# The chunk loop of a linear recurrence with two MLP stages: its steps in another order

## The chip, the cores and the metric

The kernel runs on one core of a Trainium2 chip. The metric is the device time of one execution in microseconds; the time before is the median of three runs.

## The reference

Two things follow each other. The first is a recurrence over 768 time steps, for 4 x 8 heads with a 40 x 40 state each:

```python
for t in range(S):
    y[:, :, t] = np.einsum('bhd,bhde->bhe', rt, state)
    Sa = np.einsum('bhde,bhe->bhd', state, at)
    state_decay = state * wt[:, :, None, :] - np.einsum('bhd,bhe->bhde', Sa, bt)
    state = state_decay + np.einsum('bhd,bhe->bhde', vt, kt)
```

Its output, 3072 tokens of 320 features, goes through two MLPs: `elu(x @ w_in) @ w_out` with 2048 hidden features, then `max(x @ w1, x @ w2, x @ w3) @ w_out` with 768 hidden features. All is in fp32 (the weights come as 64-bit numbers).

## The kernel before, in words

The recurrence is done in 24 chunks of 32 time steps. In a chunk, the 32 heads lie side by side in small blocks, and the steps inside the chunk are solved as a triangular system. The first MLP runs beside it: TensorE works on its 128 x 256 pieces between the small steps of the recurrence. The second MLP runs when the recurrence has ended.

Every engine takes its instructions in the order in which the program writes them (`tc.manual_schedule()`), so the order of calls in the chunk loop is the order of each engine's queue. A chunk `c` has eight segments `s0` to `s7`. In segment `n` these are written one behind another:

- the segment's own steps, `s()`;
- `KP[n]` steps of the generator `stK(c + 1)`, which turns the K and B data of the next chunk (tile KT) into YL: per half one 32 x 32-block transpose on VectorE (tile psK in PSUM), then four steps of two copies each on ScalarE; at `n == 5` what is left of it is flushed, and the next KT is loaded;
- what `CHAIN` says for the loads, stores and statistics of the triangular solve, which itself runs on GpSimd;
- where `n` is in `LT` (from chunk 4 on), one tick of `later`, the conversion of the second MLP's weights: four ticks a weight piece, each of one or two VectorE passes, some with a DMA, a sum of absolute values (Abs) on ScalarE, or both;
- two fills: one `fc1` (eight matmuls into `h`, then an exp on ScalarE and, for an older piece, a cast) and one `fc2` (six matmuls into `acc`, then two VectorE passes on an `e`, called elu here, and a subtraction on GpSimd).

The steps of the recurrence in chunk `c` are, with `d = c + 2`:

- `stU`, `stT1`, `stX`, `stT2`, `stS`: the chain of the state. psU is copied to Us by ScalarE, psV likewise to v; psX is added to Us by VectorE (L337); psT is copied to VSI by ScalarE (four copies); psS is multiplied into US by VectorE (four passes, L358).
- `stR(c, h)`: transposes one half of US through psR, in two tiles of eight, and ScalarE copies them (L371) into YL of the next chunk. psS of the next chunk reads them.
- `stN`: transposes VSI through psN; ScalarE copies it to VN. `stG` multiplies VN with Rbd, VectorE masks the result into GR. `stY` and `stY2` make the output of the chunk before (Yt on VectorE, then a split into two parts and DMAs to DRAM).
- `prep1a`, `prep1b`, `prep2`, `prep3`, `prep_stat`: scans (Q, Pt), the products Abd (one half for each of two values of `par`, L177) and KT (two halves, L185) on VectorE, and two passes with an accumulated sum over Q and Pt on ScalarE (L195).
- `stA(d, h)`: multiplies KT with Abd into psA; VectorE masks psA into AK (L201), then ScalarE copies parts to NB and Abd to AK.

All PSUM tiles of the recurrence (psU, psV, psX, psT, psA, psK, psS, psR, psN, psG, psY) share four buffers of the pool `ps`. The tiles h have two buffers, acc two.

Of the kernel before, what the change touches and what calls it, by code (L numbers as in the profile page):

```python
# [7 lines left out]
F32 = mybir.dt.float32  # L8
# [25 lines left out]
ST = ((3, 3, 2, 3, 3, 2, 3, 3), (2, 2, 3, 3, 3, 3, 4, 4))  # L34
NW = 8
NF = 8
LT = (1, 3, 4, 6, 7)
N3, N1 = 34, 22
NPC = N3 + N1
KD = 3  # L40
K0 = (0, 0, 2, 2, 2, 2, 2, 2)
KP = (0, 1, 1, 1, 2, 1, 2, 2)
FL = ((0, 0, 0, 0, 2, 2, 2, 2), (2, 2, 2, 2, 2, 2, 2, 2), (2, 2, 2, 2, 2, 2, 2, 2), (2, 2, 2, 2, 2, 2, 2, 2))


# [11 lines left out]
def _main(tc, io, out, bad):  # L57
# [4 lines left out]
    with ExitStack() as outer, tc.manual_schedule():  # L62
# [27 lines left out]
        r1 = rec.enter_context(tc.tile_pool(name="r1", bufs=1))  # L90
# [23 lines left out]
        def load_wa(c):  # L114
            if c < NCH:
                wa = r1.tile([104, 1056], F32, tag="wa", name="wa")
                sp.dma_start(wa[:], io["wa"][c])
                wt[c], at[c] = wa, wa[:, 544:]
# [10 lines left out]
        def load_vsi(c):  # L129
            if c < NCH:  # L130
                sp.dma_start(VSI[0:32].rearrange("p a b e -> p (a b e)"), io["vt"][c])
# [41 lines left out]
        def prep2(c, par):  # L173
            if c >= NCH:
                return
            sl = slice(64 * par, 64 * par + 40)
            nc.vector.tensor_tensor(  # L177
                out=Abd[sl, par], in0=at[c][sl, :].rearrange("p (a b) -> p a b", b=32),
                in1=Pt[c][sl, :, 0:32], op=mult,
            )  # L180
# [50 lines left out]
        def stK(c):  # L231
            if c >= NCH:
                return
            new_YL(c)
            for h in range(2):
                if c < KD:
                    q = [ps.tile([64, 8, 40], F32, tag="ps", name="psK") for _ in range(2)]
                    for p in range(8):
                        for par in range(2):
                            sl = slice(64 * par, 64 * par + 40)  # L240
                            nc.tensor.transpose(q[par][:, p], KB[c][sl, 8 * h + p].rearrange("r a b -> r (a b)"),
                                                ident[sl, sl])
                    yield
                    for par in range(2):
                        nc.scalar.copy(YL[c][0:64, 8 * h:8 * h + 8, par], q[par][:])
                        yield
                    continue
                q = ps.tile([128, 8, 2, 32], F32, tag="ps", name="psK")
                nc.vector.transpose(out=q[:].rearrange("r p k t -> r (p k t)"),  # L249
                                    in_=KT[c % 2][:, 8 * h:8 * h + 8].rearrange("r p k t -> r (p k t)"))  # L250
                yield
                for par in range(2):
                    for e0, n in ((0, 32), (32, 8)):
                        for k in range(2):
                            nc.scalar.copy(YL[c][32 * k:32 * k + 32, 8 * h:8 * h + 8, par, e0:e0 + n],  # L255
                                           q[64 * par + e0:64 * par + e0 + 32, :, k, 0:n])
                        yield
# [54 lines left out]
        def stU(c):  # L312
            q = ps.tile([128, 8, 40], F32, tag="ps", name="psU")
            for g in range(8):
                for k in range(4):
                    par, p = head(k, g)
                    nc.tensor.matmul(q[32 * k:32 * k + 32, g], AK[c][:, par, p], US[:, p, par],
                                     start=True, stop=True)
            QQ["us"] = us = r1.tile([128, 8, 40], F32, tag="Us", name="Us")
            nc.scalar.copy(us[:], q[:])  # L320
# [13 lines left out]
        def stX(c):  # L334
            q = ps.tile([128, 8, 40], F32, tag="ps", name="psX")
            blocks(q, NB[c % 3], QQ["v1"], 16)
            nc.vector.tensor_tensor(out=QQ["us"][:], in0=q[:], in1=QQ["us"][:], op=add)  # L337
            nc.scalar.activation(out=QQ["v1"][:, :, 0:32], in_=NB[c % 3][:], func=ACTF.Abs,
                                 accum_out=stat[:, c, 4:5])
# [8 lines left out]
        def stS(c, h):  # L348
            if c + 1 >= NCH:
                return  # L350
            q = ps.tile([104, 8, 40], F32, tag="ps", name="psS")
            for p in range(8):
                for par in range(2):
                    nc.tensor.matmul(q[64 * par:64 * par + 40, p], YL[c][:, 8 * h + p, par],
                                     VSI[:, 8 * h + p, par], start=True, stop=True)
            for par in range(2):
                sl = slice(64 * par, 64 * par + 40)
                nc.vector.tensor_tensor(  # L358
                    out=US[64:104, 8 * h:8 * h + 8, par], in0=q[sl],
                    in1=PC[c + 1][sl, 8 * h:8 * h + 8].to_broadcast([40, 8, 40]), op=mult,  # L360
                )
# [11 lines left out]
        def stN(c):  # L373
            q = ps.tile([80, 16, 32], F32, tag="ps", name="psN")
            for p in range(16):
                nc.tensor.transpose(q[:, p], VSI[32:64, p].rearrange("r a e -> r (a e)"), ident[32:64, 32:64])
            nc.scalar.copy(VN[:, :, 1], q[:])
# [364 lines left out]
        for c in range(NCH):  # L742
            d = c + 2 if c else NCH
            def s0():
                if c:
                    stU(c)
                    stY(c - 1)
                    load_gr(c)
                load_us(c + 1)
                prep1b(d)  # L750

            def s1():
                stT1(c)
                if c:
                    stY2(c - 1)
                prep2(d, 0)
                prep2(d, 1)

            def s2():
                stX(c)  # L760
                load_wa(d + 1)
                prep3(d, 0)
                prep3(d, 1)

            def s3():
                stT2(c)
                stA(d, 0)
                stA(d, 1)

            def s4():  # L770
                stS(c, 0)
                stS(c, 1)
                load_vsi(c + 1)

            def s5():
                stN(c)
                prep_stat(d)

            def s6():
                stR(c, 0)  # L780
                stG(c, 0)
                stG(c, 1)
                load_g(c + 1)

            def s7():
                stR(c, 1)
                prep1a(c + 3)

            segs = (s0, s1, s2, s3, s4, s5, s6, s7)
            if c == 3:  # L790
                qw[0] = sp
            sk = stK(c + 1)
            for n, s in enumerate(segs):
                if c == 2 and n == LX:
                    tick(99)
                    tick(1, second)
                if n == 2 and c >= 2 and c % 2 == 0:
                    state["x", c // 2 - 1] = load_x(c // 2 - 1)
                if n == (DN if c > 2 else D2) and c >= 2 and c % 2 == 0:
                    done[0] = c // 2  # L800
                if c > 1 and n == 3:
                    for _ in sv:
                        pass
                    solve_store(c + 1)
                s()
                for _ in range(KP[n] if c + 1 >= KD else K0[n]):
                    next(sk, None)
                if n == 5:
                    for _ in sk:
                        pass  # L810
                    load_kb(c + 3)
                for f, k in CHAIN[min(c, 2)].get(n, ()):
                    chain[f](c + k)
                if c < 2:
                    if ("load", 2) in CHAIN[c].get(n, ()):
                        for _ in solve(c + 2):
                            pass
                else:
                    if n == 7:
                        sv = solve(c + 2)  # L820
                if c < 2 or c == 2 and n < LX:
                    tick(FT[c][n])
                elif c < 4:
                    tick(ST[c - 2][n], second)
                if c == 3 and n == 7:
                    tick(1, later)
                if c > 3 and n in LT:
                    tick(1, later)
                for _ in range(FL[(c > 2) + (c > 3) + (c == NCH - 1)][n] if c > 1 else 0):
                    fill()  # L830
                    next(sv, None)
                    next(sv, None)
# [362 lines left out]
```

## Time and profile before

| | |
|---|---|
| median of three runs | 1109.33 us (1108.91 to 1109.74) |
| the profiled execution, its time | 1110.41 us |
| its span, first to last instruction | 1108.5 us |
| TensorE matmul busy | 968.2 us (87%) |
| VectorE busy | 702.3 us (63%) |
| ScalarE busy | 587.2 us (53%) |
| GpSimd busy | 443.0 us (40%) |
[...]

Busy shares are means over the whole span. The chunk loop is over at about 760 us, the rest of the first MLP at about 826 us, and behind that lies the second MLP. In the profile PE is the matmul engine, PEld its weight load, DVE is VectorE, ACT ScalarE, POOL GpSimd, SP the queue that issues most DMAs. Names such as L337 are lines of the kernel. A releaser, behind "<-", is the instruction whose end let the waiting one start.

### The profile page before, as it was taken

The page shows a single profiled execution, that of the slowest core. Times are in us where ns is not written, and L with a number is a line of the kernel's source. Part 1 is how long each engine was busy: PE and PEld are TensorE (multiplying, and loading weights), DVE is VectorE, ACT ScalarE, POOL GpSimd, SP SyncE. Part 2 cuts the span into 40 slices and gives each one's busy share as a digit, 9 for nine tenths or more (in the row PEclk, how much of TensorE's full clock was granted, in tenths as well). Part 3 has the DMA queues.
Part 4 walks back from the last instruction along what each step waited for, and adds up shares of the span by engine and source line. Part 5 has one row for each costly group of instructions (what it writes and reads, how often), then busy time and mean ns, then how long its engine had stood idle before and what let it go on. Part 6 is the DMA issues. An engine that isn't in the chain of part 4 may idle for free.

```text
span 1108.5 us, 38422 instructions
## 1 busy us (share of the span) xinstructions
PE 968.2 (87%) x15992; PEld 863.5 (78%) x15992; DVE 702.3 (63%) x1368; ACT 587.2 (53%) x1705; POOL 443.0 (40%) x952
## 2 busy tenths in 40 slices
PE   2255697998999988899999898999999999999996
PEld 2154587888888887788888887888998888888885
DVE  7979786777777877877677777775433333333321
ACT  3466655776776666667667666775332212122121
POOL 3542264665656666655556666653330000000000
PEclk9965578999998999999889999999999999999998
DMA  6854554664555556545545555542581001010000
GB/s 170 218 149 128 128 138 97 158 144 118 138 149 138 139 139 153 140 116 126 141 121 146 131 137 143 142 125 74 178 231 28 29 26 53 1 53 24 1 24 27
DMA packets 187430, 125.27 MB, mean 113 GB/s; under 512 B 125770, under 2 KB 167498, under 8 KB 187122
## 3 DMA queue, kind: packets, MB, share of 16 engines
q1 hardware_dynamic: 174123, 104.66, 37.8%
q10 hardware_dynamic: 13127, 18.09, 5.4%
q8 instruction: 128, 2.10, 0.8%
q14 instruction: 52, 0.43, 0.1%
HBM read 92.82 MB, written 29.88 MB: 111 GB/s over the span
## 4 chain that ended last, share of the span: by engine, by line
PE 45%; DVE 27%; DMA 8%; ACT 8%; issue 4%; POOL 4%; SPq 2%; ACTq 0%; POOLq 0%; DVEq 0%
PE psh L881 18%; PE h L566 7%; PE acc L600 6%; PE acc L903 5%; ACT YL L255 3%; PE psA L215 3%; DVE e L578 3%; DVE e L577 2%; DVE US L358 2%; DVE Abd L177 2%; DVE KT L185 2%; DVE Yt L398 2%; DVE Pt L166 2%; DVE psK L249 2%; DVE AK L201 2%
## 5 line engine op out<-in xcount | busy, mean ns | idle before, releaser
L566 PE MATMUL h<-x,W 128*128 128x256 f32 x1536 | 243.6, 303 | 12.4 <-DMA x<-dX 6.7
L587 POOL TENSOR_TENSOR g<-e,g 128x256 fp32r<-128x256 f32 x192 | 156.8, 817 | 237.1 <-DVE e L577 108.5
L566 PEld LDWEIGHTS h<-x,W 128*128 128x128 f32 x1536 | 204.9, 197 | 23.2 <-issue 8.3
L881 PE MATMUL psh<-xT,V 128*128 128x512 f32 x864 | 212.3, 397 | 0.8 <-ACT xT L872 0.7
L600 PE MATMUL acc<-W2h,g 128*128 128x320 f32 x768 | 204.4, 315 | 0.4 <-POOL g L587 0.4
L881 PEld LDWEIGHTS psh<-xT,V 128*128 128x128 f32 x864 | 159.4, 188 | 34.9 <-ACT xT L872 1.0
L284 POOL TENSOR_TENSOR tmp<-WT,X 128x15 f32<-128x15 f32 (+4 forms) x360 | 125.4, 348 | 97.9 <-ACT raw L443 25.9
L577 DVE TENSOR_SCALAR e<-e 128x256 f32<-128x256 f32 x192 | 69.5, 362 | 143.4 <-ACT e L570 143.3
L886 DVE TENSOR_TENSOR mx<-psh,mx 128x512 f32<-128x512 f32 x72 | 49.8, 692 | 159.2 <-PE psh L881 159.1
L600 PEld LDWEIGHTS acc<-W2h,g 128*128 128x128 f32 x768 | 140.8, 194 | 3.2 <-issue 2.0
L286 POOL TENSOR_TENSOR WT<-WT,tmp 128x15 f32<-128x15 f32 (+4 forms) x360 | 129.7, 360 | 28.2
L600 PE MATMUL acc<-W2l,g 128*128 128x320 f32 x384 | 121.0, 315 | 2.4 <-issue 2.4
L889 ACT CAST g<-mx 128x512 fp32r<-128x512 f32 x36 | 22.3, 620 | 173.1 <-DVE mx L886 173.1
L570 ACT ACTIVATE e<-h 128x256 f32<-128x256 f32 x192 | 73.5, 383 | 72.4 <-PE h L566 47.9
L255 ACT COPY YL<-psK 32x256 f32<-32x256 f32 (+1 forms) x336 | 95.2, 283 | 30.1 <-DVE psK L249 25.9
L578 DVE TENSOR_TENSOR e<-h,e 128x256 f32<-128x256 f32 x192 | 81.5, 425 | 6.6
L215 PE MATMUL psA<-Abd,KT 104*64 104x64 f32 x768 | 46.1, 278 | 39.8 <-DVE KT L185 37.3
L583 ACT CAST g<-e 128x256 fp32r<-128x256 f32 x192 | 76.3, 398 | 0.6 <-DVE e L578 0.3
L600 PEld LDWEIGHTS acc<-W2l,g 128*128 128x128 f32 x384 | 74.6, 194 | 0.0
L215 PEld LDWEIGHTS psA<-Abd,KT 104*64 104x64 f32 x768 | 39.6, 186 | 44.4 <-ACT W L468 21.6
L903 PE MATMUL acc<-O,g 128*128 128x320 f32 x432 | 69.2, 308 | 0.1
L903 PEld LDWEIGHTS acc<-O,g 128*128 128x128 f32 x432 | 66.2, 188 | 3.5 <-DVE g L890 0.4
(123 smaller groups left out, 1468.0 us busy)
## 6 DMA issues: line engine op xcount, KB each, us to landing
wa<-in_wa SPq DMA_DIRECT2D x24, 429.0 KB
KT<-in_kbT SPq DMA_DIRECT2D x23, 416.0 KB
rawv<-in_wv SPq DMA_DIRECT2D x18, 384.0 KB
X<-dN SPq DMA_DIRECT2D x96, 64.0 KB
x<-dX SPq DMA_DIRECT2D x24, 256.0 KB
V<-dV SPq DMA_DIRECT2D x6, 960.0 KB
raw<-in_w ACTq DMA_DIRECT2D x7, 768.0 KB
US<-in_vt SPq DMA_DIRECT2D x24, 160.0 KB
```

The lines of the kernel that those rows point to most:

```text
L215: nc.tensor.matmul(q[64 * u:64 * u + 64, p], KB[c][:, 8 * u + p].rearrange("r a b -> r (a b)"), Abd[:, :, 8 * u + p], start=True, stop=True)
L255: nc.scalar.copy(YL[c][32 * k:32 * k + 32, 8 * h:8 * h + 8, par, e0:e0 + n], q[64 * par + e0:64 * par + e0 + 32, :, k, 0:n])
L284: eng.tensor_tensor(out=tv, in0=Wt[:, 0:nu, s:s + 1].to_broadcast([128, nu, n]), in1=X[:, s:s + 1, s + 1:16].to_broadcast([128, nu, n]), o ...
L286: eng.tensor_tensor(out=Wt[:, 0:nu, s + 1:16], in0=Wt[:, 0:nu, s + 1:16], in1=tv, op=sub)
L566: nc.tensor.matmul(h, W1[:, wi, 128 * m:128 * m + 128], x[:, xi], start=(n == 0), stop=(n == 7))
L577: nc.vector.tensor_scalar(out=e[:], in0=e[:], scalar1=1.0, scalar2=-1.0, op0=ALU.min, op1=add)
L578: nc.vector.tensor_tensor(out=e[:], in0=h, in1=e[:], op=ALU.max)
L583: nc.scalar.copy(gt[i][:, 0], es[i][:])
L587: nc.gpsimd.tensor_tensor(out=gt[i][:, 1], in0=es.pop(i)[:], in1=gt[i][:, 0], op=sub)
L600: nc.tensor.matmul(acc[t][:], g[:, gi, ts], w[:, m], start=(m == 0 and n == 0), stop=(m == 15 and n == 2))
L881: nc.tensor.matmul(q[:], V[:, w, wi, ms], xT[:, hl, k], start=(n == 0), stop=(n == 7))
L903: nc.tensor.matmul(acc[t], g[:, gi, ts], O[:, wi, m], start=(m == 0 and n == 0), stop=(m == 5 and n == 2))
```

## The change

- The transposes of KT write to a tile `ks` in SBUF, with one buffer, in place of a PSUM buffer of `ps`.
- The second half of Abd (`prep2(d, 1)`) moves from segment 1 to segment 2, behind `stX`.
- `stN` moves from segment 5 to the end of segment 4, behind both halves of `stS`.
- The second half of `stR` moves from segment 7 to the start of the next chunk's segment 0.
- The steps of `stK` are spread otherwise: segment 3 has two and segment 4 one, and the flush goes from segment 5 to segment 7. The load of the next KT stays at segment 5.
- The ticks of the weight conversion stand in segments 2, 4, 5, 6, 7 in place of 1, 3, 4, 6, 7.

```diff
--- before.py
+++ after.py
@@ -34,12 +34,12 @@
 ST = ((3, 3, 2, 3, 3, 2, 3, 3), (2, 2, 3, 3, 3, 3, 4, 4))
 NW = 8
 NF = 8
-LT = (1, 3, 4, 6, 7)
+LT = (2,4,5,6,7)
 N3, N1 = 34, 22
 NPC = N3 + N1
 KD = 3
 K0 = (0, 0, 2, 2, 2, 2, 2, 2)
-KP = (0, 1, 1, 1, 2, 1, 2, 2)
+KP = (0, 1, 1, 2, 1, 1, 2, 2)
 FL = ((0, 0, 0, 0, 2, 2, 2, 2), (2, 2, 2, 2, 2, 2, 2, 2), (2, 2, 2, 2, 2, 2, 2, 2), (2, 2, 2, 2, 2, 2, 2, 2))
 
 
@@ -245,7 +245,7 @@
                         nc.scalar.copy(YL[c][0:64, 8 * h:8 * h + 8, par], q[par][:])
                         yield
                     continue
-                q = ps.tile([128, 8, 2, 32], F32, tag="ps", name="psK")
+                q = r1.tile([128, 8, 2, 32], F32, tag="ks", name="ks")
                 nc.vector.transpose(out=q[:].rearrange("r p k t -> r (p k t)"),
                                     in_=KT[c % 2][:, 8 * h:8 * h + 8].rearrange("r p k t -> r (p k t)"))
                 yield
@@ -743,6 +743,7 @@
             d = c + 2 if c else NCH
             def s0():
                 if c:
+                    stR(c - 1, 1)
                     stU(c)
                     stY(c - 1)
                     load_gr(c)
@@ -754,10 +755,10 @@
                 if c:
                     stY2(c - 1)
                 prep2(d, 0)
-                prep2(d, 1)
 
             def s2():
                 stX(c)
+                prep2(d, 1)
                 load_wa(d + 1)
                 prep3(d, 0)
                 prep3(d, 1)
@@ -770,10 +771,10 @@
             def s4():
                 stS(c, 0)
                 stS(c, 1)
+                stN(c)
                 load_vsi(c + 1)
 
             def s5():
-                stN(c)
                 prep_stat(d)
 
             def s6():
@@ -783,7 +784,6 @@
                 load_g(c + 1)
 
             def s7():
-                stR(c, 1)
                 prep1a(c + 3)
 
             segs = (s0, s1, s2, s3, s4, s5, s6, s7)
@@ -806,9 +806,10 @@
                 for _ in range(KP[n] if c + 1 >= KD else K0[n]):
                     next(sk, None)
                 if n == 5:
+                    load_kb(c + 3)
+                if n == 7:
                     for _ in sk:
                         pass
-                    load_kb(c + 3)
                 for f, k in CHAIN[min(c, 2)].get(n, ()):
                     chain[f](c + k)
                 if c < 2:
```

## Rows read from the trace of the kernel before

**Rows 1.** stretches: from:to, length, PE PEld DVE ACT POOL busy, clock, DMA, GB/s
```profile
184.60:733.10 548.50, 502.13 (x10950) 455.30 (x10948) 418.15 (x801) 376.39 (x1143) 330.44 (x706) 0.95 0.55 135
704.90:733.10 28.20, 26.24 (x592) 23.65 (x588) 21.73 (x46) 21.05 (x66) 17.80 (x42) 1.00 0.54 129
733.10:758.70 25.60, 25.20 (x580) 22.95 (x580) 18.73 (x39) 16.72 (x51) 15.08 (x37) 1.00 0.49 130
```

**Rows 2.** waits of TensorE, 200 to 780 us: total us, times, longest
```profile
PE psT L326 <- DVE Us L337: 21.1, 14, 2.8
PE psR L370 <- ACT YL L371: 8.5, 13, 0.7
PE psA L215 <- DVE KT L185: 5.3, 13, 0.7
```

**Rows 3.** waits of VectorE, 200 to 780 us
```profile
DVE e L577 <- ACT e L570: 114.6, 47, 3.6
DVE AK L201 <- PE psA L215: 17.1, 17, 1.4
```

**Rows 4.** timeline of VectorE, 591 to 615 us: start, us, what, idle before
```profile
599.06 0.29 DVE L577 TENSOR_SCALAR e<-e 128x256 f32<-128x256 f32 x1 [2.40 <-ACT e L570]
...
601.89 0.70 DVE L448 SCALAR_TENSOR_TENSOR cf<-rawv 128x384 fp32r<-128x384 f32 x1
...
603.18 0.72 DVE L249 STREAM_TRANSPOSE psK<-KT 128x512 f32<-128x512 f32 x1
606.72 0.29 DVE L577 TENSOR_SCALAR e<-e 128x256 f32<-128x256 f32 x1 [2.83 <-ACT e L570]
```

**Rows 5.** timeline of ScalarE, 591 to 615 us
```profile
598.20 0.42 ACT L255 COPY YL<-psK 32x64 f32<-32x64 f32 x2
598.64 0.38 ACT L570 ACTIVATE e<-h 128x256 f32<-128x256 f32 x1
...
599.49 1.18 ACT L255 COPY YL<-psK 32x256 f32<-32x256 f32 x4
...
601.26 0.59 ACT L377 COPY VN<-psN 80x512 f32<-80x512 f32 x1
601.74 0.65 ACT L195 ACTIVATE Q<-Q 104x528 f32<-104x528 f32 x1
...
603.92 2.35 ACT L255 COPY YL<-psK 32x256 f32<-32x256 f32 x8 [0.68 <-DVE psK L249]
```

**Rows 6.** chain that ended last, 520 to 650 us: start, us, what
```profile
593.20 1.16 PE psA L215 x30
...
619.26 1.62 DVE rawv L436
...
623.91 1.74 PE psA L215 x30
```

**Rows 7.** groups by line: busy us, mean ns, idle before
```profile
L185 DVE TENSOR_TENSOR KT<-KT,Q 104x512 f32<-104x512 f32 x48 | 40.5, 883 | 0.1
...
L177 DVE TENSOR_TENSOR Abd<-wa,Pt 40x512 f32<-40x512 f32 x48 | 35.8, 747 | 0.3
...
L225 ACT COPY AK<-Abd 40x512 f32<-40x512 f32 x48 | 29.6, 617 | 0.8
...
L377 ACT COPY VN<-psN 80x512 f32<-80x512 f32 x24 | 14.0, 582 | 4.3 <-PE psN L376 4.3
```

**Rows 8.** timeline of TensorE, 591 to 615 us
```profile
602.45 0.75 PE L370 MATMUL psR<-ident,US 40*40 40x40 f32 x16
```

**Rows 9.** timeline of TensorE, 556 to 572 us
```profile
561.31 0.79 PE L326 MATMUL psT<-Us,TB 32*32 32x40 f32 x64 [1.88 <-DVE Us L337]
...
563.04 1.97 PE L215 MATMUL psA<-Abd,KT 104*64 104x64 f32 x30 [0.68 <-DVE KT L185]
564.95 2.08 PE L566 MATMUL h<-x,W 128*128 128x256 f32 x8
...
570.34 1.22 PE L566 MATMUL h<-x,W 128*128 128x256 f32 x8
```

## The prediction

> **What bounds the kernel now.** I read the stretches first. The steady chunks c = 4 to 21 take 184.6 to 733.1 us [rows 1]: 548.5 / 18 = 30.47 us a chunk. After that TensorE is all but full (25.20 us busy of 25.60 in chunk 22 [rows 1]) and nothing there is touched, so a gain has to come out of those 18 chunks. The chunk from 704.9 ran wholly at the full clock and was 28.20 us long with 26.24 us of TensorE work [rows 1]; TensorE therefore could do a chunk in some 26.3 us, and about 4.2 us of each chunk are waits and half clock.
>
> The waits of TensorE tell where [rows 2], over 19 chunks: psT for Us (the psX add on VectorE) 21.1 us, psR for a copy of an older psR 8.5, psA for KT 5.3. It looks as if the late add were the fault. But why is VectorE late? Its own waits [rows 3] are 114.6 us, 6.0 a chunk, for the exp on ScalarE. The timeline of one chunk names two places [rows 4]: 2.40 us before the elu of segment 3 and 2.83 us before that of segment 5. ScalarE's timeline [rows 5] shows what it did meanwhile: before the first it runs the copies of AK and then two of YL, before the second the flush of eight YL copies, 2.35 us from 603.92, which stand in its queue ahead of segment 5's exp.
>
> So I read the chunk as a ring on VectorE and ScalarE. The chain of waits runs from psA at 593.20 to psA at 623.91 [rows 6], 30.71 us: psA, AK masks (VectorE), NB and AK copies, YL copies, exp (ScalarE), elu, US, convert tick, elu, psK transpose (VectorE), YL flush, exp (ScalarE), then without a break on VectorE elu, GR, tick, elu, Q, tick, elu, Yt, Pt, elu, Abd, psK, tick, elu, the add, KT, and psA again. What shortens this ring shortens the chunk; what only moves TensorE's wait within it does not.
>
> **The change part by part**, costed in this ring.
>
> *The add above Abd's second half.* The add now comes one Abd half (0.75 us [rows 7]) sooner, and the tick that stood ahead of it is gone from segment 1. psT starts earlier and its wait shrinks. But psA needs the second Abd half and both KT products (0.88 us each [rows 7]), and these now stand behind the add: VectorE runs the same instructions before psA as before. In the ring: 0. TensorE's wait goes from psT to psA.
>
> *The YL flush leaves segment 5.* The exp of segment 5 no longer stands behind eight copies. VectorE's 2.83 us go, if that exp is ready when VectorE gets there. In the row's chunk ScalarE now ends exp and cast of segment 3 at 599.49, where the next copies start, and would end them at 599.49 + 0.90 = 600.4 (the 0.90 is the next two items). Then come VN 0.59, a YL pair 0.42, exp and cast of segment 4 some 0.7, both statistics 603.92 - 0.68 - 601.74 = 1.50 and an exp 0.38 [rows 5]: ready at 604.0. VectorE would be there at 603.18 + 0.72 [rows 4] + 0.90 = 604.8 plus a tick. The margin is 0.8 us and the tick. Gain 2.83. The copies go to segments 6 and 7, where ScalarE loses no time of VectorE: the exps are wanted there after GR, Q and ticks.
>
> *One more YL step in segment 3.* KP[3] becomes 2, so one more pair, 1.18 - 0.42 = 0.76 us [rows 5], runs ahead of the exp for which VectorE already waits 2.40. Loss 0.76.
>
> *KT's transposes into SBUF.* ScalarE now reads its source from SBUF. The nearest pair of rows, both 512 elements, is 617 ns from SBUF against 582 from PSUM [rows 7]: 35 ns a copy, four in segment 3, loss 0.14; the other twelve lie in cover. [...] The transpose itself on VectorE, 0.72 us into PSUM [rows 4], has no row into SBUF. Bounds: 0.56 (an SBUF to SBUF pass over 256 elements takes 0.29 [rows 4], doubled) and 0.88 (KT, two SBUF inputs, 512 elements [rows 7]). It streams one input of the same 512 elements, so I take 0.72; two of them in the ring make the range +-0.32 a chunk.
>
> *The ticks.* Segments 1, 3, 4, 6, 7 become 2, 4, 5, 6, 7. The one in 1 moves to 5: both lie in the ring, 0. The one in 3 ran inside the 2.40 us wait, free; in 2 it stands between KT and the AK masks, where VectorE waits for psA 17.1 / 17 = 1.0 us [rows 3]. A tick takes 0.70 to 1.62 us and more [rows 4, 6], about 1.0 on average; where psA is quick it spills over. Loss 0 to 0.6, taken 0.3. The tick's weight load (SP) and stores (ScalarE's queue) move with it by one or two segments; a piece is loaded one piece, four ticks, ahead, so nobody waits.
>
> *psN beside psS; psR's second half in the next chunk.* psN's 16 transposes and the VN copy move up; 16 transposes of psR, 0.75 us [rows 8], and two copies move into the next chunk's start, ahead of psU. Neither issues a DMA, and GpSimd's and SP's queues keep their order. The next half of psR no longer waits for a PSUM buffer, nor does KT's transpose hold one: TensorE's 8.5 us [rows 2] go, but TensorE is not the ring, and the gain is 0. Behind the moved copies on ScalarE stand Us and the exp of segment 0; VectorE gets to that exp only after Yt and Pt. If that cover were gone they would cost two copies, some 0.8 us.
>
> Sum: 2.83 - 0.76 - 0.14 - 0.3 = 1.63 us a chunk; 18 x 1.63 = 29.3. Chunks 2 and 3 share the order but are full of weight conversion: between 0 and 2 each, taken 0.5. Chunks 0, 1, 22, 23 and all behind: 0. Together 30 us. The profiled execution took 1110.4 us (span 1108.5 and 1.9 around it), 1.1 above the median; 1110.4 - 30 = 1080.4, less 1.1 is **1079**.
>
> **The clock.** [...] The granted clock of 0.95 over the 18 chunks [rows 1] means some 10% of the time at half. [...] I leave the clock's share as it is: a slow chunk puts psA 0.8 later in the ring, but raises TensorE's work by about 3 us, which takes away the next chunk's wait. Never slow would gain 0.4 a chunk (7 us), always slow lose 0.5 (9 us).
>
> **The rivals.**
> *A, the exp of segment 5 stays late* (a statistics pass and a tick's Abs ahead of it, ScalarE late from segment 3). The margin is 0.8 us and a tick; if the exp is 1 us later than VectorE, 0.6 a chunk is left, 11 us: 1098. For it: the tick now in segment 5 puts work on ScalarE in one chunk of four.
> *B, TensorE becomes the bound.* If the ring is looser than I read it, a chunk falls to 26.3 to 27: 18 x 3.5 to 4.2 = 63 to 75 us, 1034 to 1046. Against it: VectorE's ring has 28.8 us of work and waits that this change leaves. [...]
> *C, slower: the single SBUF buffer.* The second transpose must wait until ScalarE has copied out the last of the first. Now ScalarE would end those at 601.4 and VectorE be there at 604.1: 2.7 us spare. From there each us of lateness adds one to the ring; at 2.7 + 1.6 = 4.3 us the gain is gone, and at 5 us a chunk is 0.7 longer: 1122. For it: VN's copy now precedes those copies and waits for TensorE's psN; against it, psN runs one h and acc pair earlier than now, and ScalarE asks for it at 600.4, not at 601.26 [rows 5].
> *D, no change*: the 2.83 us wait moves whole to segment 3 or 0: 1107 to 1111.
>
> **How the numbers follow.** Forecast 0.62: with the transposes' and the tick's bounds and the clock's, 1065 to 1093. A 0.18, B 0.06, C 0.09, D 0.05. The range 1055 to 1100 takes in A and leaves out B, C and D, 0.2. Faster by over 0.2% (2.2 us, about what three runs can tell) 0.86, same 0.05, slower 0.09.
>
> **What would show it.** In the profile after: a steady chunk of 28.8 us; VectorE's wait for the exp at 3 to 3.5 us in segment 3 and nearly none in 5; TensorE's wait for Us mostly gone and that for KT risen to 1.5 us or more a chunk; no wait of psR; YL copies 35 ns longer; the transpose near 0.72 us. I am wrong if the transpose or TensorE's psU waits for ScalarE's copies, if segment 5's exp is still waited for, or if the chunk falls under 28 us.

## The result, and the profile after

After: 1099.68 us in the median of 20 runs (1084.58 to 1107.74); before, timed beside it, 1109.53 (1100.92 to 1121.99, 20 runs). The ratio is 0.986, with a 95% interval of 0.9834 to 0.9885; it leaves out the runs that lie over 1.5% above the fastest of their kernel, 8 of the 20 after and 1 of the 20 before, which is why it is not that of the two medians. The ratio makes 15.5 us of 1109.5, about half of the 30 forecast; the medians of all runs lie 9.9 us apart, a third of it. The profiled execution took 1093.44 us, 17.0 less than that of before.

The stretches first, as in [rows 1]: all 18 steady chunks, chunks 4 to 13, 14 to 20, and 21 (from:to, length, busy us of PE, PEld, DVE, ACT, POOL, clock, DMA share, GB/s). After:

```profile
182.01:716.81 534.80, 489.59 (x10956) 446.17 (x10952) 405.34 (x799) 390.76 (x1142) 321.38 (x705) 0.97 0.57 139
182.01:470.91 288.90, 267.15 (x6086) 243.10 (x6082) 225.57 (x442) 216.93 (x635) 179.02 (x390) 0.99 0.57 143
470.91:686.50 215.59, 195.42 (x4298) 178.27 (x4292) 158.84 (x314) 151.99 (x444) 123.84 (x271) 0.94 0.56 135
686.50:716.81 30.31, 27.02 (x588) 24.80 (x584) 20.93 (x45) 21.84 (x64) 18.52 (x45) 0.94 0.55 132
```

The same view of before, chunks 4 to 13 and 14 to 20:

```profile
184.55:486.92 302.37, 277.53 (x6086) 251.51 (x6087) 231.62 (x444) 209.01 (x634) 185.09 (x393) 0.96 0.56 137
486.92:704.88 217.96, 198.40 (x4287) 180.17 (x4288) 164.83 (x313) 146.35 (x445) 127.58 (x273) 0.94 0.53 133
```

Here is the whole riddle. Chunks 4 to 13 fell to 28.89 us each, and 28.8 was forecast: 13.5 us gained of 16.3. Chunks 14 to 20 still took 215.59 / 7 = 30.80 us each: 2.4 gained of 11.4 (the forecast's 1.63 us a chunk). Chunk 21 was 2.1 us longer than before [rows 1], where 1.6 less was forecast. Something else sets the later chunks.

The waits of TensorE, 200 to 740 us (total us, times, longest), against [rows 2]:

```profile
PE psV L326 <- DMA TB<-dT: 19.4, 8, 4.3
PE h L566 <- DVE e L578: 5.3, 19, 0.3
...
PE psA L215 <- DVE KT L185: 1.8, 6, 0.3
```

psT no longer waits for Us, and psR no longer waits. New, and on top, is a wait of psV for TB, the result of the triangular solve that comes back through DRAM (L294 stores it to dT, L300 fetches it). The waits of VectorE in the same stretch:

```profile
DVE e L577 <- ACT e L570: 101.6, 32, 4.4
DVE Us L337 <- PE psX L326: 10.3, 11, 2.3
DVE AK L201 <- PE psA L215: 5.4, 7, 1.9
```

[rows 3] goes on to 780 us; before, in these same 540 us, the wait for the exp was

```profile
DVE e L577 <- ACT e L570: 100.8, 37, 3.6
```

So in total VectorE waited for the exp as long as before, but in other places. Counted by place, segment 3 went from 48.5 to 74.4 us and segment 5 from 51.8 (18 waits) to 1.0 (one wait). New are 24.6 us, in 11 waits, in segment 1 of the next chunk, where before there was one of 0.5.

In the timeline of VectorE, 366 to 385 us, against [rows 4], the wait for the exp stands once, in segment 3 (372.63); that of segment 5 (377.47) has none:

```profile
372.63 0.29 DVE L577 TENSOR_SCALAR e<-e 128x256 f32<-128x256 f32 x1 [4.19 <-ACT e L570]
...
376.61 0.70 DVE L249 STREAM_TRANSPOSE ks<-KT 128x512 f32<-128x512 f32 x1
...
377.47 0.83 DVE L577 TENSOR_SCALAR e<-e 128x256 f32<-128x256 f32 x1
```

Now the queue that the prediction left out. Timeline of SP after, 485 to 502 us (chunk 14), with L294 the dT stores, L272 the loads of the next solve's X, L300 the fetch of TB:

```profile
485.68 0.92 SPq L117 DMA_DIRECT2D wa<-in_wa  x1
486.70 8.45 SPq L294 DMA_DIRECT2D dT<-WT  x4
495.24 0.40 SPq L222 DMA_DIRECT2D dN<-AK  x1
497.98 2.85 SPq L272 DMA_DIRECT2D X<-dN  x4
500.92 0.37 SPq L131 DMA_DIRECT2D VSI<-in_vt  x1
501.33 0.57 SPq L300 DMA_DIRECT2D TB<-dT  x1
```

GpSimd's timeline, 480 to 506 us (the solve before ends, the next begins):

```profile
486.46 0.21 POOL L286 TENSOR_TENSOR WT<-WT,tmp 128x8 f32<-128x8 f32 x1
...
502.42 0.21 POOL L284 TENSOR_TENSOR tmp<-WT,X 128x15 f32<-128x15 f32 x1 [5.21 <-DMA X<-dN]
```

and TensorE's, 495 to 512 us:

```profile
505.86 0.78 PE L326 MATMUL psV<-Us,TB 32*32 32x40 f32 x64 [4.25 <-DMA TB<-dT]
506.57 1.86 PE L566 MATMUL h<-x,W 128*128 128x256 f32 x8
```

Read together, this is a second ring. The solve ends at 486.67, its four dT stores are issued from 486.70 on but take SP until 495.15, then come the dN store and, when that has landed, the X loads (497.98). The next solve waits 5.21 us for them, starts at 502.42, and its dT stores start at 517.49: 8.54 + 2.74 + 4.44 + 15.07 = 30.79 us from dT to dT in this pass, where the first ring takes 28.9. The TB fetch stands in SP's queue behind the X loads, so psV waits as well, and the eight h matmuls after the wait run mostly at half the full clock (1.86 us against 1.22 [rows 9], with a granted clock of 0.58; before, from 562.9 to 569 us, it was 0.50). From there the delay reaches the first ring: ScalarE's copy of v waits for psV, its next exp comes late, and VectorE waits for that exp in segment 1. ScalarE and VectorE, 500 to 514 us:

```profile
506.69 0.43 ACT L332 COPY v<-psV 128x320 f32<-128x320 f32 x1 [4.54 <-PE psV L326]
...
508.95 1.41 DVE L577 TENSOR_SCALAR e<-e 128x256 f32<-128x256 f32 x1 [4.42 <-ACT e L570]
```

The second ring does not lead in every pass. Over 200 to 740 us the solve waited for X 12 times and dT for the solve 9 times, in 18 chunks. TensorE's eight waits for TB fall in every second chunk: 5.8 us in the four before 490 us, 13.5 in the four after. Nor does its slack run out steadily. The first X load was issued 22.8 us after the chunk's start (ScalarE's copy of Us, L320) in chunk 4, 26.4 in chunk 6, 27.1 in chunk 14, 25.5 in chunk 16 and 30.8 in chunk 20. Why the waits are longer in the late chunks is not shown.

What kept the dT stores? The waits of SP, 200 to 740 us, after:

```profile
SPq L294 <- POOL WT L286: 41.3, 9, 6.0
SPq L272 <- DMA dN<-AK: 34.0, 18, 2.7
SPq L294 <- DMA dV<-cf: 22.1, 4, 8.0
...
SPq L294 <- DMA dV<-cx: 19.1, 3, 8.9
```

The wait for the solve (WT) must be there. The waits for dV, the weight stores of the ticks, are not data waits: dT and dV share nothing. The trace shows where they come from. The 839 DMAs of this program, those of SP and of ScalarE together, tell their landing on eight semaphores, taken in turn (104 or 105 DMAs each). In each of the eight holds of dT by a weight store (with one for dO, 45.0 us), the dT store uses the semaphore of the very store that it waits for, and was issued 0.01 to 0.02 us after the last landing of that store. So these waits stand in the program's own instructions. In chunk 14 three of the four dT stores went out at once. The record of the fourth waits for semaphore 101 and tells its own landing on 101 too; it waited 6.8 us for a store with 101 that ScalarE, busy with copies and exps, issued only at 491.84 (timelines of ScalarE, 484 to 512 us, and of SP, 494.5 to 495.3):

```profile
491.84 0.32 ACTq L519 DMA_DIRECT2D dV<-cf  x1
...
494.84 0.30 SPq L294 DMA_DIRECT2D dT<-WT  x1
```

So the second ring runs through ScalarE too, and is not independent of the first.

### The profile page after: what moved, and what is told of

Its sections match the earlier page's. It is cut to its first block, busy times and chain, and to the rows that moved or that the text cites. A ratio compares the mean times of both kernels' runs of the same rounds, so it can differ in the third digit from the quotient of the medians.

```text
span 1091.7 us, 38353 instructions
## 1 busy us (share of the span) xinstructions
PE 960.2 (88%) x15992; PEld 858.7 (79%) x15992; DVE 686.3 (63%) x1368; ACT 603.6 (55%) x1705; POOL 432.2 (40%) x952
## 4 chain that ended last, share of the span: by engine, by line
PE 55%; DVE 20%; DMA 8%; ACT 8%; issue 5%; POOL 2%; SPq 1%; ACTq 0%; POOLq 0%; DVEq 0%
PE psh L882 18%; PE h L566 11%; PE acc L600 8%; PE acc L904 6%; DMA TB<-dT 3%; DVE AK L201 3%; ACT YL L255 2%; DVE KT L185 2%; ACT NB L221 2%; DVE e L578 2%; DVE e L577 2%; PE psA L215 2%; PE psR L370 2%; DVE Abd L177 2%; PE psY L394 2%
## 5 line engine op out<-in xcount | busy, mean ns | idle before, releaser
L566 PE MATMUL h<-x,W 128*128 128x256 f32 x1536 | 243.3, 303 | 13.5 <-DVE e L578 11.8
L587 POOL TENSOR_TENSOR g<-e,g 128x256 fp32r<-128x256 f32 x192 | 150.6, 785 | 203.1 <-ACT g L583 143.2
L286 POOL TENSOR_TENSOR WT<-WT,tmp 128x15 f32<-128x15 f32 (+4 forms) x360 | 123.0, 342 | 28.2
L255 ACT COPY YL<-ks 32x256 f32<-32x256 f32 (+1 forms) x336 | 108.5, 323 | 6.1 <-DVE ks L249 1.4
L570 ACT ACTIVATE e<-h 128x256 f32<-128x256 f32 x192 | 73.2, 381 | 65.3 <-PE h L566 45.5
L215 PE MATMUL psA<-Abd,KT 104*64 104x64 f32 x768 | 36.8, 245 | 37.3 <-DVE KT L185 32.9
L215 PEld LDWEIGHTS psA<-Abd,KT 104*64 104x64 f32 x768 | 31.7, 155 | 41.0 <-ACT W L468 20.7
```

The costliest lines, as they stand in the source:

```text
L215: nc.tensor.matmul(q[64 * u:64 * u + 64, p], KB[c][:, 8 * u + p].rearrange("r a b -> r (a b)"), Abd[:, :, 8 * u + p], start=True, stop=True)
L286: eng.tensor_tensor(out=Wt[:, 0:nu, s + 1:16], in0=Wt[:, 0:nu, s + 1:16], in1=tv, op=sub)
L566: nc.tensor.matmul(h, W1[:, wi, 128 * m:128 * m + 128], x[:, xi], start=(n == 0), stop=(n == 7))
L587: nc.gpsimd.tensor_tensor(out=gt[i][:, 1], in0=es.pop(i)[:], in1=gt[i][:, 0], op=sub)
```

## The experiments

Ratios are to the kernel before, timed beside each on the same chip.

| | ratio | 95% interval |
|---|---|---|
| the change | 0.986 | 0.9834 to 0.9885 |
| flush_only | 0.976 | 0.971 to 0.981 |
| no_flush | 1.0077 | 1.0047 to 1.0108 |
| fetch_first | 1.0188 | 1.0139 to 1.0236 |
| tick_phase | 0.9798 | 0.9747 to 0.9849 |
| old_ticks | 0.9747 | 0.9711 to 0.9784 |
| add_below | 0.9869 | 0.9823 to 0.9915 |
| fewer_dma | 0.9606 | 0.9569 to 0.9644 |
| flush_fewer | 0.9679 | 0.9635 to 0.9724 |
| fewer_old_ticks | 0.9594 | 0.9557 to 0.963 |
| loads_scalar | 0.9845 | 0.9808 to 0.9882 |
| x_four | 0.9727 | 0.969 to 0.9764 |
| pair_later | 0.9523 | 0.9486 to 0.956 |

**flush_only**: the kernel before with `ks` in SBUF, the new `KP` and the flush in segment 7; nothing else.

```diff
-KP = (0, 1, 1, 1, 2, 1, 2, 2)
+KP = (0, 1, 1, 2, 1, 1, 2, 2)
-                q = ps.tile([128, 8, 2, 32], F32, tag="ps", name="psK")
+                q = r1.tile([128, 8, 2, 32], F32, tag="ks", name="ks")
                 if n == 5:
+                    load_kb(c + 3)
+                if n == 7:
                     for _ in sk:
                         pass
-                    load_kb(c + 3)
```

> The kernel before with three edits alone: KT's transposes into SBUF, the new spread of the copies (KP) and their flush in segment 7. The add, psN, psR and the ticks stay where they were. Ring theory (VectorE waits for the exp of segment 5 behind the flush): the wait of 2.83 us in segment 5 goes, one more pair of copies in segment 3 costs 0.9, the tick of segment 3 stays hidden: 1.9 us a chunk, as much as the whole change or more in the chunks where nothing else is late, so 1075 to 1095. Rival (TensorE's wait for the late add is what counts): the add is as late as before, only TensorE's waits of psR go, 1100 to 1110.

Measured 0.976, 26.6 us less: the late flush alone gives more than the whole change. The rest of the change costs 1%.

**no_flush**: the change with `KP` and the flush as before.

```diff
-KP = (0, 1, 1, 2, 1, 1, 2, 2)
+KP = (0, 1, 1, 1, 2, 1, 2, 2)
                 if n == 5:
-                    load_kb(c + 3)
-                if n == 7:
                     for _ in sk:
                         pass
+                    load_kb(c + 3)
```

> The changed kernel with the copies of KT's transposes spread and flushed as before (KP of before, flush in segment 5), all other edits kept. Ring theory: the wait of 2.83 us is back, the earlier add is worth nothing, the tick of segment 2 costs up to 0.3 a chunk: 1105 to 1117. Rival (the earlier add and TensorE's waits are what counts): most of the gain stays, 1090 to 1100.

Measured 1.0077. Without the flush, all else that the change does, the earlier add with it, is a loss of 8.5 us. Both runs speak for the ring on VectorE and ScalarE, and against the rival of their expectations, that TensorE's wait for the late add is what counts.

**fetch_first**: the change, with the fetch of TB ahead of the X loads.

```diff
-S2 = {0: (('stat', 0),), 1: (('init', 2),), 3: (('load', 2),), 4: (('fetch', 1),)}
+S2 = {0: (('stat', 0),), 1: (('init', 2),), 3: (('fetch', 1), ('load', 2))}
```

> The changed kernel with the load of TB put ahead of the loads of X in SP's queue (segment 3, as soon as dT is stored). Theory of the new wait (in the changed kernel psV waits for TB, 19.4 us in 200 to 760 us, and TensorE's clock falls behind it; TB stands on SP behind X and its wait for dN): TB lands some 2.5 us sooner, psV's wait for it falls from 19.4 us to under 6, the later chunks come down from 31 to about 29 us, and the time falls by 8 to 20 us against the changed kernel, to 1078 to 1088. Rival (the gain was mis-sized in the ring, TB's wait only takes the place of another): as the changed kernel within 0.4%.

Measured 1.0188, a miss as a cure. TensorE's waits, 200 to 740 us:

```profile
PE acc L600 <- POOL g L587: 36.0, 31, 1.9
PE h L566 <- DMA x<-dX: 10.1, 9, 3.0
PE psV L326 <- DMA TB<-dT: 3.7, 4, 1.9
```

and GpSimd's:

```profile
POOL g L587 <- ACT g L583: 106.5, 52, 6.1
POOL tmp L284 <- DMA X<-dN: 83.7, 16, 9.1
```

The wait for TB fell from 19.4 to 3.7 us, but the fetch has to wait for dT to land (SP 30.4 us in that stretch), the X loads stand behind it, and the solve's wait for X rose from 36.6 to 83.7. GpSimd is then late with everything. So TB is only where the second ring shows; the ring itself runs through X and the solve.

**tick_phase**: the change, with one tick more at the end of chunk 3, so that each tick kind falls elsewhere.

```diff
                 if c == 3 and n == 7:
-                    tick(1, later)
+                    tick(2, later)
```

> The changed kernel with one more tick of the weight conversion ahead of chunk 4, so that the kinds of tick swap between even and odd chunks: in even chunks, which also load x, segment 2 then holds a tick without DMAs. Theory (the weight DMAs of segment 2, issued just before dT, delay dT and so TB in even chunks): psV's wait for TB falls by half or more, 1080 to 1090. Rival (the x and wa loads alone delay dT, or only SP's order behind X does): no difference to the changed kernel beyond 0.4%.

Measured 0.9798: about 0.6% better than the change, intervals overlapping. Weight stores held dT for 35.2 us there, 4.7 at most, against 45.0 and 8.9. Which DMAs share a semaphore may matter; the run doesn't show that this is the cause.

**old_ticks**: the change with the ticks where they were.

```diff
-LT = (2,4,5,6,7)
+LT = (1, 3, 4, 6, 7)
```

> The changed kernel with the ticks of the weight conversion in segments 1, 3, 4, 6, 7 as before; all other edits kept. Theory of two rings: in the ring of VectorE and ScalarE the tick of segment 3 is hidden again and those of 1 and 5 cancel, 0 to 0.3 us a chunk; in the ring of SP and GpSimd (dT stored, dN, X loaded, solve, dT again) no weight DMA is issued any more between the load of wa and dT, so dT and TB come sooner: 1078 to 1090, near the run with the flush alone. Rival (the ticks do not matter): as the changed kernel within 0.4%. Rival (the tick ahead of the add costs): slower than the changed kernel by 5 us or more.

Measured 0.9747: the moved ticks cost 0.9860 - 0.9747 = 0.0113, 12.5 us, or 0.70 us a chunk where the prediction took 0.3. The wait for TB fell to 11.5 us, the waits of dT for weight stores from 45.0 to 37.7 (in both, cf and cx of dV and dO together).

**add_below**: the change with both halves of Abd above the add again.

```diff
                 prep2(d, 0)
+                prep2(d, 1)
 
                 stX(c)
-                prep2(d, 1)
```

> The changed kernel with both halves of Abd in segment 1 again, ahead of the psX add; all other edits kept. Ring theory: VectorE runs the same work ahead of psA either way, TensorE's wait goes from psA to psT: within 0.5% of the changed kernel; the load of wa, which waits for Abd's second half, and dT behind it on SP come a little sooner, so rather faster than slower. Rival (the early add is worth its 0.75 us a chunk): 13 us slower than the changed kernel.

Measured 0.9869 against 0.986: the early add is worth nothing here, as forecast, while the second ring's waits are there (TensorE waits 34.9 us for TB).

**fewer_dma**: the change with less in SP's queue: x comes in four transfers in place of six, in every second chunk, and dT goes out in two in place of four. The same bytes move.

```diff
-            for z in range(4):
-                o = 16 - 16 * (z // 2)
-                sp.dma_start(dT[c][:].rearrange("(b u w) h t -> b w h u t", b=2, w=2)[z // 2, z % 2],
-                             WT[c % 2][32 * z:32 * z + 32, :, o:o + 32])
+            for b in range(2):
+                o = 16 - 16 * b
+                sp.dma_start(dT[c][:].rearrange("(b u w) h t -> b (w h) u t", b=2, w=2)[b],
+                             WT[c % 2][64 * b:64 * b + 64, :, o:o + 32])
...
-            sp.dma_start(xb[0:64, 4], dX[b][0, 256:320])
-            sp.dma_start(xb[64:128, 4], dX[b][0, 256:320])
-            sp.dma_start(xb[0:64, 5], dX[b][1, 256:320])
-            sp.dma_start(xb[64:128, 5], dX[b][1, 256:320])
+            for p in range(2):
+                sp.dma_start(xb[64 * p:64 * p + 64, 4:6], dX[b][:, 256:320].rearrange("l r n -> r l n"))
```

> The changed kernel with x loaded by four DMAs in place of six and dT stored by two in place of four, the same bytes. Theory of the second ring (SP's queue between one dT and the next sets the later chunks): SP has some 0.9 us less to issue in every chunk and 1.2 more in every second one, and dT waits for fewer earlier DMAs; psV's wait for TB (19.4 us) falls to half or less and the time by 6 to 14 us against the changed kernel. Rival (the bytes of x and wa, not their number, hold dT back): no change beyond 0.4%.

Measured 0.9606. No engine's arithmetic changed, and 2.5% came off. SP's waits there, 200 to 740 us:

```profile
SPq L294 <- POOL WT L286: 50.8, 17, 5.5
SPq L272 <- DMA dN<-AK: 36.6, 14, 4.7
SPq L272 <- DMA dV<-cx: 21.6, 5, 6.7
```

The profile is of the slowest of the six runs (1078.3 us; median 1067.6). dT now waits for the solve alone. The waits for weight stores have not gone: 45.5 us of them (cx and cf, of dV and dO) stand at the X loads, one step on in SP's queue. But dT and dN are out of the way sooner, and the solve's wait for X fell from 36.6 to 5.8 us, the wait for TB from 19.4 to 2.9. The edit does two things at once: SP has less to issue, and with 767 DMAs in place of 839, other DMAs meet on the same semaphore. No run separates the two. The kernel before with the same shorter queue wasn't run either, so it isn't known how much of the 2.5% that kernel would have gained.

**flush_fewer**: flush_only with the two edits of fewer_dma.

> The kernel with the flush alone, with the same fewer DMAs. Second ring: this kernel's psV also waited for TB (12.5 us in 200 to 740 us), so it gains 5 to 10 us against the flush alone, 1073 to 1080, ahead of both kernels. Rival: as the flush alone within 0.4%.

Measured 0.9679, 0.8% less than flush_only, with intervals that just overlap: the second ring seems to bite there too, but less.

**fewer_old_ticks**: fewer_dma with the old `LT`.

> The change with the ticks back in their old segments and with fewer transfers on SP's queue (x loads 6 to 4 a block, dT stores 4 to 2 a chunk). Alone the old ticks gave a ratio of 0.975 and the fewer transfers 0.961, against 0.986 for the change. If both took away the same thing, the length of the ring through SP's queue and GpSimd, then together they give no more than the better one: 0.956 to 0.962 (1061 to 1067 us). If the ticks' new places cost VectorE's ring by themselves, the two add up: 0.986 - 0.011 - 0.025 = 0.950 (1054 us).

Measured 0.9594 against 0.9606: the two cures don't add up. What the moved ticks cost in the change is the second ring's doing; beside the shorter queue they cost nothing that can be told.

**loads_scalar**: the change, with the ticks' weight loads on ScalarE's queue.

```diff
-            if c == 3:
-                qw[0] = sp
```

> The change, but the weight loads that the ticks issue stay on ScalarE's queue in every chunk; nothing else differs, and VectorE's ticks are where the change puts them. If the moved ticks cost through SP's queue (a weight load ahead of the dT store and the fetch of TB), the time falls to that of the old ticks, 0.975 (1082 us) or below, and TensorE's waits for TB fall under 10 us of 540. If they cost on VectorE, the ratio stays 0.986 (1094 us) or rises, since ScalarE now holds the loads.

Measured 0.9845, as the change. So it is not the place of the weight loads in SP's queue alone. ScalarE lost by holding them: VectorE's wait for the exp rose from 101.6 to 118.5 us and TensorE's for TB from 19.4 to 34.5. What SP gained is not told apart from that.

**x_four**: the x part of fewer_dma alone.

> The change with the x loads alone cut from 6 transfers to 4 a block; the dT stores stay 4 a chunk. Both cuts together gave 0.961 against 0.986. If what counts is the number of transfers that stand in SP's queue ahead of the dT store, and x is loaded in every second chunk only, about half of it comes from here: 0.973 (1080 us), with the long even chunks shorter. If the dT stores themselves are the long part (two landing instead of four), it stays near 0.986; if the x loads are all of it, 0.961.

Measured 0.9727, on the expected half: some 1.3% from the x loads, and 1.2% more with the dT stores.

**pair_later**: fewer_dma with the extra YL pair back in segment 4; the flush stays in segment 7.

```diff
-KP = (0, 1, 1, 2, 1, 1, 2, 2)
+KP = (0, 1, 1, 1, 2, 1, 2, 2)
```

> The change with fewer transfers on SP's queue, and the extra pair of YL copies back from segment 3 to segment 4 (the flush stays in segment 7). The forecast gave this pair 0.76 us a chunk in the ring, so with the second ring out of the way: 18 x 0.76 = 13.7 us less than with the fewer transfers alone, a ratio of 0.949 (1053 us). If the copies only make ScalarE late one segment further on, where the margin of segment 5 was 0.8 us, the ratio stays at 0.961 (1066 us) and VectorE's wait for the exp moves from segment 3 to segment 5.

Measured 0.9523, 53 us less than before and the best of all. It is 0.0083, 9.2 us, under fewer_dma, 0.51 us a chunk where the term was 0.76. The stretches, chunks 4 to 13 and 14 to 20:

```profile
179.59:455.76 276.17, 264.97 (x6088) 242.80 (x6085) 229.31 (x442) 216.50 (x634) 184.82 (x392) 0.99 0.61 150
455.76:652.40 196.64, 184.07 (x4276) 169.33 (x4272) 161.63 (x314) 151.47 (x445) 126.81 (x271) 1.00 0.61 149
```

27.6 and 28.1 us a chunk, no step from the early to the late ones, the full clock in both. In VectorE's timeline, 440 to 462 us, the exp wait of segment 3 is 3.35 us where the change has 4.19; none follows in segment 5:

```profile
444.45 0.29 DVE L575 TENSOR_SCALAR e<-e 128x256 f32<-128x256 f32 x1 [3.35 <-ACT e L568]
```

and SP's timeline, 440 to 470 us, has the dT stores in 1.31 us and X right behind the landing of dN:

```profile
442.21 1.31 SPq L294 DMA_DIRECT2D dT<-WT  x2
443.62 0.58 SPq L222 DMA_DIRECT2D dN<-AK  x1
446.66 2.13 SPq L272 DMA_DIRECT2D X<-dN  x4
```

## Why the prediction was right, and where its size was off

The sign, the ring on VectorE and ScalarE and the place of its main term were right. The size was half by the ratio, a third by the medians. That 1099.68 lies in the stated range is luck: the range ends at 1100 because it takes in rival A (1098), and A's mechanism did not happen.

By the runs, the missing 14 to 15 us stand in two places. The three flush edits were forecast at 2.83 - 0.76 - 0.14 = 1.93 us a chunk, 34.7 in 18, and flush_only gave 26.6. The ticks were forecast at 5.4 and cost 12.5.

- *The flush leaves segment 5, 2.83 us.* Right: the wait is gone in 17 of 18 chunks (1.0 us is left in one), and flush_only gives 26.6 us by itself. Rival A (the exp stays late) didn't happen.
- *The extra YL pair, 0.76 us.* Right in place. The exp wait of segment 3 is 4.19 us with the pair and 3.35 without, 0.84; by the times 0.51. The sign named for that wait, 3 to 3.5 us, was missed: the moved tick no longer fills it. With the old ticks it is 3.6 behind a tick of about 0.6 us (L448).
- *SBUF source, 35 ns a copy.* The YL copies went from a mean of 283 to 323 ns, 40 ns. The transpose takes 0.70 us into SBUF (0.72 taken), and it waits for the single buffer once in the whole execution, 0.8 us, and not from 200 to 740 us: rival C fell.
- *The early add, psN, psR: 0.* Right in the change itself (add_below 0.9869; old_ticks 0.9747 beside flush_only 0.976). Beside the shorter queue these edits together give 0.9594 against 0.9679, some 0.8%: a zero in a sum may hold only while another ring covers it.
- *psA waits for KT, 1.5 us or more a chunk.* Wrong: 1.8 us in all, and VectorE's waits for psA fell from 17.1 [rows 3] to 5.4. TensorE's remaining waits stood at psV instead, for TB.
- *The clock left as it is.* About so: 0.95 [rows 1] became 0.97 over the 18 chunks, 0.99 in the early ones and 0.94 in the late ones, where the waits for TB are. In pair_later, with 1.8 us of those waits in 540, it is 1.00 there. Over the whole span 0.931 of the full clock became 0.937; the traces before and after hold two levels, 1.00 and 0.50. The 3 us of more work in a slow chunk, and the 0.4 and 0.5 us a chunk of the range, were the author's estimate, and no run shows them.
- *The ticks.* This step failed. "The tick's weight load (SP) and stores (ScalarE's queue) move with it by one or two segments; a piece is loaded one piece, four ticks, ahead, so nobody waits", and for the rest "GpSimd's and SP's queues keep their order". Both look for a wait on data. SP, which carries dT, X and TB of the solve, waited at dT for those very stores to land, 45.0 us in 540, up to 8.9 at a time, since the program has them share semaphores. The term was taken at 0.3 us a chunk and measured 0.70.
- *One ring.* Behind that lies the larger omission: the sum let one ring set all 18 chunks. The ring of SP and GpSimd (dT, dN, X, solve) was not costed, though timelines of SP and GpSimd before were there to cost it from. SP's waits there, 200 to 740 us, already had this:

```profile
SPq L294 <- POOL WT L286: 32.8, 9, 4.4
...
SPq L294 <- DMA dV<-cf: 17.5, 3, 6.2
...
SPq L300 <- DMA dV<-cx: 13.7, 3, 5.4
```

With 30.5 us a chunk the second ring had room: TensorE never waited for TB in these 540 us, and the solve waited 8.7 us for X. With 28.9 it has not in every second chunk, most of all from chunk 14 on. fewer_dma and x_four show that fewer DMAs there give back 2.5% and 1.3%; that this is the missing half of the forecast, and not in part a gain that the kernel before would have had as well, is not shown.

Rival B, TensorE as the bound, did not come, though TensorE is the busiest engine (489.59 of 534.80 us after): the chunks took 28.89 and 30.80 us, not 26.3 to 27. TensorE's work was never touched in these runs, and the time went from 1.0188 to 0.9523 with the order and number of items in two queues; at 27.6 us a chunk against 26.5 of TensorE work (264.97 / 10) in pair_later, it does come next.

Open: why one more tick at the start (tick_phase) helps, and how much of the 2.5% comes from fewer issues and how much from other pairs on the eight semaphores. Giving dT a semaphore that no weight store uses would separate them; that wasn't tried. It stays open as well why the moved ticks cost nothing beside the shorter queue.

## What to carry to other kernels

When the instructions of each engine run in a written order, look for every ring that closes from chunk to chunk, those through a DMA queue and DRAM too, and cost the second longest before you promise what shortening the longest will give. Of a moved step that issues DMAs, ask which later item of any queue may have to wait until they have landed, also without common data: look up which DMAs share a semaphore (here 45.0 us of SP's waits in 540). A queue that only issues can lead: here four DMAs fewer in a chunk with x loads and two in one without gave 2.5% with all arithmetic unchanged.

## What was unexpected of the hardware

- A held issue held its whole queue. In the 6.8 us in which the fourth dT store waited for ScalarE's weight store, SP issued nothing; it was issued at 494.84, and all that stood behind it on SP came after: dN at 495.24, X at 497.98, TB at 501.33.
- Two products of unchanged shape changed their mean duration with their place. Over 200 to 740 us Abd (L177) went from 729 to 834 ns and KT (L185) from 930 to 755. The shortest of each stayed (673 ns before and after; 681 and 691), the longest went from 1141 to 1554 and from 1525 to 1659: a few long ones make the means.

What else was running beside them would be the place to look; that wasn't tried.
